# First routing in lots between attention tiles, and one expert's second products behind the last table product, in a fused attention and mixture kernel

## The chip, the cores and the metric

The kernel runs on one core of a Trainium2 chip. The core has a matrix engine (PE, with its weight loads as PEld), a vector engine (DVE), an activation engine (ACT), a general engine (POOL) and a queue engine (SP) that mostly starts transfers. The metric is the device time of one execution in microseconds (us), as the median of several runs.

## What is computed

The reference runs three stages in a row: an attention through 32 memory slots a head, a mixture of eight experts of which each token uses two, and a dense layer with a cosine gate.

```python
a = softmax(phi); k_m = a^T k; v_m = a^T v              # per batch and head, 32 slots
attn = softmax(q k_m^T / sqrt(64)); x = attn v_m        # 2304 tokens x 512
logits = x @ w_gate + log1p(exp(x @ w_noise)) * noise   # 2304 x 8
for e in range(8):                                      # the two best experts of each token
    h = np.maximum(x[mask] @ w1[e], 0.0)                # 512 -> 1024
    out[mask] += top2_w[mask, k, None] * (h @ w2[e])    # 1024 -> 512
h = out @ w_in; g = h * np.cos(h); return g @ w_out     # 512 -> 2048 -> 512
```

Every number is float32 outside. Inside, the expert and dense products are float16 in high and low parts, three products for one.

## The kernel before

The 2304 tokens are 18 tiles of 128. **The attention** makes the keys and values of four batches (k_gen) and then runs each tile through t_gen: scores sc on PE; maximum and difference (smx, sd) on DVE; exp on ACT; sum and reciprocal (ssm) on DVE, recorded as last["t7V"] for tile 7; the product d on POOL; two transposes pt on PE and their copy e2T on ACT; the products x on PE ("t7P"); the copy xs and the routing's logits on ACT ("t7A"); and a high and low half hl, which SP stores to xd. There is one x buffer, so x of a tile waits for the copy of the tile before. The values of the last batch go through the one PSUM bank "kt" as pk, pv and vn, and so do the sums of the first two weights.

**The routing** (route) runs twice, over the tokens of tiles 0 to 7 and of tiles 8 to 17. It is a chain on DVE with two short functions on ACT: two best experts, a rank product on PE (rank), and then tables: for each tile two one-hot matrices (ohp, oha) on DVE and two table products on PE (tab). From the table of the first run comes idxA, from both comes idxB. They drive the gathers of an expert's first part (two tiles of 128 tokens) and second part (three tiles): POOL gathers rows of xd into xg, SP transposes them into x. Then PE makes h (l1) and y (l2).

**Each weight** is loaded as float32 in two halves (raw), squared in four pieces on ACT (w_square, instructions junk), summed by PE (sum_up, sums) and turned into a scale on DVE (wnm, wnt, wsc). Then ACT writes four high parts (w_hi) and DVE four low parts (w_lo). Weights 0 and 1 are those of the first expert, w1 and w2.

**Order.** Every step is put on a line of times with at(t, ...), which gives it a priority; a scheduler then fixes the order on each engine. `gated(key)` forces an instruction behind a recorded one on the same engine, and `chain` keeps a kind of work in its order. So the first routing was one step at R0, put at the time of tile 13 with lots of 99; the pieces of both weights were gated behind tiles 7 to 17; and the y products of the first expert's first part were gated behind rank and the tables 2, 5 and 8:

```python
at(R0, advance, r0, 99)
at(tA + 0.01 + 0.001 * c, l2, 0, c, (("rank", "tab2"), ("tab5", "tab8"))[c], lead=LA)
```

In the profile most instructions that go through `chain` carry line 219, so one goes by their tiles.

## Time and profile before

| | us |
| --- | --- |
| median of 3 runs | 952.22 (951.37 to 953.31) |
| the profiled execution | 951.91 |
| its span, first to last instruction | 950.1 |
| PE busy in it | 894.6 |
| DVE, ACT, POOL busy | 583.9, 468.5, 213.1 |

The profile is one execution. Busy PE is not PE at its best: PEclk tells the share of the full clock that was granted in a stretch. Engines run side by side, and each takes its instructions in a fixed order, so an instruction can wait for something that it doesn't need because one ahead of it does. A row of a timeline has the start, the length, the engine, the line, the operation with the tiles written and read, the count, and in brackets the idle time before it and what ended that.

### The profile page before, as it was taken

What the parts mean: (1) busy time and instruction counts of PE and PEld (TensorE: products, weight loads), DVE (VectorE), ACT (ScalarE), POOL (GpSimd) and SP (SyncE); (2) the same over time, 40 slices, a digit from 0 to 9 for tenths busy, and PEclk for the clock granted to TensorE, in tenths of its full rate; (3) what the DMA queues carried; (4) which work ended last, traced back from release to release, by engine and by line L of the source; (5) the groups of instructions that cost most, each with busy time, mean ns of one, the idle gap of its engine ahead of it and who ended that gap; (6) DMA issues with size and microseconds to landing.
All of it is one profiled execution on the core that took longest, in us unless ns stands there. A gap on an engine that the chain in (4) does not pass through costs nothing. (4 is left out here: it accounts for less than half of the span.)

```text
span 950.1 us, 14147 instructions
## 1 busy us (share of the span) xinstructions
PE 894.6 (94%) x5368; PEld 521.2 (55%) x5368; DVE 583.9 (61%) x1266; ACT 468.5 (49%) x830; POOL 213.1 (22%) x234
## 2 busy tenths in 40 slices
PE   4996795999999999999998999989999999999997
PEld 3775463574746565564745555655444444444564
DVE  2568561385766567576763338887885774555564
ACT  3487523567666676667772324444433433332242
POOL 1353302201010201001000114443522432322222
PEclk8796597999999999999999999999999999999999
DMA  9972308858877879988753273231400320200010
GB/s 353 396 265 103 77 33 266 260 172 288 264 234 263 196 274 286 300 231 292 264 178 134 79 242 70 78 77 34 112 11 12 109 59 0 77 13 1 1 45 23
DMA packets 108246, 146.55 MB, mean 154 GB/s; under 512 B 65808, under 2 KB 66448, under 8 KB 106128
## 3 DMA queue, kind: packets, MB, share of 16 engines
q1 hardware_dynamic: 89536, 103.56, 35.1%
q0 software_dynamic: 6080, 19.93, 7.3%
q10 hardware_dynamic: 12560, 22.13, 6.6%
q8 instruction: 43, 0.70, 0.3%
q14 instruction: 27, 0.22, 0.1%
HBM read 95.26 MB, written 35.13 MB: 137 GB/s over the span
## 5 line engine op out<-in xcount | busy, mean ns | idle before, releaser
L219 PE MATMUL h<-x,w 128*128 128x384 f16 (+1 forms) x1536 | 216.0, 302 | 10.8 <-DMA x<-xg 10.6
L219 PE MATMUL y<-w,hT 128*128 128x512 f16 x960 | 212.7, 381 | 4.0 <-issue 4.0
L219 PE MATMUL g<-x2T,win 128*128 128x256 f16 (+1 forms) x1152 | 202.5, 326 | 5.3 <-DVE ty L1010 4.1
L219 PE MATMUL o<-wout,gT 128*128 128x512 f16 x864 | 202.0, 379 | 0.4 <-POOL gT L1012 0.2
L219 PEld LDWEIGHTS <-w 128*128 128x128 f16 x1536 | 151.9, 100 | 70.8 <-issue 13.9
L219 PEld LDWEIGHTS <-win 128*128 128x128 f16 x1152 | 112.6, 98 | 89.8 <-issue 7.6
L219 PEld LDWEIGHTS <-hT 128*128 128x128 f16 x960 | 94.3, 99 | 113.8 <-issue 6.6
L1012 POOL TENSOR_TENSOR gT<-ty,gT 128x256 f16<-128x256 f32 (+1 forms) x96 | 92.6, 965 | 252.9 <-ACT gT L1011 249.1
L1009 ACT ACTIVATE tt<-tt,hp 128x256 f32<-128x256 f32 (+1 forms) x96 | 58.9, 614 | 164.1 <-DVE tt L1008 150.1
L219 PEld LDWEIGHTS <-gT 128*128 128x128 f16 x864 | 84.2, 98 | 93.5 <-POOL gT L1012 2.2
L219 DVE SCALAR_TENSOR_TENSOR w<-raw,wsc,w 128x1024 f16<-128x1024 f32 x64 | 81.1, 1282 | 41.9 <-ACT w L219 38.3
L219 DVE SCALAR_TENSOR_TENSOR hT<-h,hT 128x384 f16<-128x384 f32 (+1 forms) x128 | 61.4, 487 | 66.6 <-ACT hT L219 66.0
L1006 DVE SCALAR_TENSOR_TENSOR ty<-g,wis,bct 128x256 f32<-128x256 f32 (+1 forms) x96 | 58.8, 612 | 65.7 <-PE g L219 65.7
L219 ACT ACTIVATE hT<-h 128x384 f16<-128x384 f32 (+1 forms) x128 | 55.4, 435 | 81.1 <-PE h L219 79.5
L1010 DVE SCALAR_TENSOR_TENSOR ty<-g,fac,tt 128x256 f32<-128x256 f32 (+1 forms) x96 | 59.1, 615 | 52.8 <-ACT tt L1009 52.1
L1011 ACT ACTIVATE gT<-ty 128x256 f16<-128x256 f32 (+1 forms) x96 | 50.2, 523 | 64.4 <-DVE ty L1010 64.3
L808 POOL DMA_INDIRECT xg<-xd,idxB x24 | 23.4, 974 | 219.9 <-DMA x<-xg 204.7
L219 ACT ACTIVATE w<-raw,wsc 128x1024 f16<-128x1024 f32 x64 | 71.6, 1140 | 2.2 <-ACT o L219 2.1
L1008 DVE SCALAR_TENSOR_TENSOR tt<-tt,ty 128x256 f32<-128x256 f32 (+1 forms) x96 | 68.9, 718 | 2.6
L219 ACT ACTIVATE junk<-raw 128x1024 bf16<-128x1024 f32 x64 | 67.5, 1054 | 3.9 <-ACT o L219 3.3
L219 ACT ACTIVATE o<-y,ysc 128x512 f32<-128x512 f32 x40 | 27.5, 686 | 75.9 <-PE y L219 64.8
L930 POOL DMA_INDIRECT y<-yd,sidx x36 | 36.1, 1003 | 91.4 <-DMA yd<-o 83.7
(234 smaller groups left out, 734.8 us busy)
## 6 DMA issues: line engine op xcount, KB each, us to landing
raw<-in_w SPq DMA_DIRECT2D x32, 1024.0 KB
yd<-o ACTq DMA_DIRECT2D x40, 256.0 KB
kvt<-in_kv SPq DMA_DIRECT2D x9, 1024.0 KB
cvt<-in_wi SPq DMA_DIRECT2D x8, 1024.0 KB
wst<-cvt SPq DMA_DIRECT2D x16, 512.0 KB
cvt<-in_wo SPq DMA_DIRECT2D x8, 1024.0 KB
yd<-zero ACTq DMA_DIRECT2D x13, 512.0 KB
xd<-hl SPq DMA_DIRECT2D x18, 256.0 KB
```

What stands on the lines that cost most here:

```text
L219: last[key] = fn(*a, **kw)
L808: G.indirect_dma_start(out=g, out_offset=None, in_=xd[0:NA * P] if part == 0 else xd, in_offset=bass.IndirectOffsetOnAxis(ap=idx[:, col:co ...
L930: G.indirect_dma_start(out=y, out_offset=None, in_=yd[0:rows], in_offset=bass.IndirectOffsetOnAxis(ap=sidx[:, t, k:k + 1], axis=0))
L1006: V.scalar_tensor_tensor(y, ph[:, :n], wis[:, 2 * E + c:2 * E + c + 1], bct[j], op0=OP.mult, op1=OP.mult)
L1008: V.scalar_tensor_tensor(t, t, MAGIC, y, op0=OP.subtract, op1=OP.subtract)
L1009: A.activation(t, t, AF.Sin, bias=hp, scale=-2.0 * math.pi)
L1010: V.scalar_tensor_tensor(y, ph[:, :n], fac[:, c:c + 1], t, op0=OP.mult, op1=OP.mult)
L1011: A.activation(g[:, 0, :n], y, AF.Copy)
L1012: G.tensor_tensor(g[:, 1, :n], y, g[:, 0, :n], op=OP.subtract)
```

## The change

The first routing is cut into lots (7, 7, 7 and the rest of its steps) at tiles 12 to 15, each lot gated behind that tile's reciprocal and behind the DVE half of the last batch's key copy. Of the first weight the squares go to tiles 7 to 10, the highs to 12 to 15, the lows behind the reciprocal of tile 17. Of the second weight the squares go behind the copies of tiles 16 and 17, the highs behind the Ln of the second routing and the lows behind idxB. The first expert's first y products go behind the last table product. The second half of the third weight's load is put behind the first gather.

```diff
@@ -436,7 +436,7 @@
             V.tensor_scalar(idxA, tb[:, :E * CA], float(TB), None, op0=OP.add)
             V.tensor_scalar(tabB, tb[:, E * CA:E * NST], float(TB), None, op0=OP.add)
         else:
-            V.tensor_tensor(idxB, tb[:, :nc_], tabB, op=OP.add)
+            last["idxB"] = V.tensor_tensor(idxB, tb[:, :nc_], tabB, op=OP.add)
         yield
         den = rg(g, "den", n)
         V.tensor_scalar(den, d, 1.0, eps, op0=OP.add, op1=OP.add)
@@ -596,7 +596,7 @@
         bk = bdk[b % 2]
         bdkt[b] = bk
         pv = pk[:, :2 * P].rearrange("p (c j m) -> p c j m", j=2, m=M)
-        V.tensor_copy(bk[0:64, :, 0:M], pv[0:64, :, 0, :])
+        last[f"bdk{b}V"] = V.tensor_copy(bk[0:64, :, 0:M], pv[0:64, :, 0, :])
         A.activation(bk[64:128, :, M:], pv[64:128, :, 1, :], AF.Copy)
         yield
         bv = ap.tile([P, 2, 272], F32, tag="bdv", name="bdv")
@@ -706,26 +706,32 @@
     k_start = (12.0, 23.0, 36.0, 46.0)
     k_steps = (-8.0, -4.0, 0.0, 4.0, 4.8, 5.4, 6.6, 7.2)
     e0_after = {
-        w_square: ("A", ((7, 7, 8, 8), (9, 9, 10, 11))),
-        w_hi: ("A", ((10, 11, 12, 12), (13, 14, 15, 16))),
-        w_lo: ("V", ((11, 12, 13, 13), (14, 15, 16, 17))),
+        (w_square, 0): ("t7A", "t8A", "t9A", "t10A"),
+        (w_hi, 0): ("t12A", "t13A", "t14A", "t15A"),
+        (w_lo, 0): ("t17V", "t17V", "t17V", "t17V"),
+        (w_square, 1): ("t16A", "t17A", "t17A", "t17A"),
+        (w_hi, 1): ("ln", "ln", "ln", "ln"),
+        (w_lo, 1): ("idxB", "idxB", "idxB", "idxB"),
     }
 
     def e0(fn, i, c):
 
-        k, after_t = e0_after[fn]
-        with gated(f"t{after_t[i][c]}{k}"):
+        with gated(e0_after[fn, i][c]):
             fn(i, c)
 
     def e0_scale(i):
-        with gated(f"t{(9, 12)[i]}P"):
+        with gated(("t11P", "t17P")[i]):
             sum_up(i, 4)
         norm_scale(i, 4)
 
-    def advance(gen, n):
-        for _ in range(n):
-            if next(gen, 1):
-                break
+    def advance(gen, n, *keys):
+
+        with ExitStack() as st:
+            for k in keys:
+                st.enter_context(gated(k))
+            for _ in range(n):
+                if next(gen, 1):
+                    break
 
     loads = [(load_phi, 0), (load_kv, 0, 2), (load_small,), (load_kv, 2, 4), (load_kv, 4, 6), (load_phi, 1),
              (load_q, 0, 4), (load_kv, 6, 10), (load_phi, 2), (load_q, 4, 8), (load_kv, 10, 14),
@@ -742,16 +748,20 @@
     for i in range(NT):
         stages(t_gen(i), [a_of(i) + x for x in t_steps])
     a_end = a_of(NT - 1) + 9.5
-    R0, R1, tA, LA = a_of(13), a_end - 0.5, a_end - 0.45, 60.0
+    R1, tA, LA = a_end - 0.5, a_end - 0.45, 60.0
     r0 = route(0)
-    at(R0, advance, r0, 99)
+    for t, n in ((12, 7), (13, 7), (14, 7), (15, 99)):
+        at(a_of(t) + 3.0, advance, r0, n, f"t{t}V", f"bdk{B - 1}V")
     whole(R1, route, 1)
-    for i in range(2):
-        for c in range(4):
-            at(a_of(e0_after[w_square][1][i][c]) + 8.5, e0, w_square, i, c)
-            at(a_of(e0_after[w_hi][1][i][c]) + 8.5, e0, w_hi, i, c)
-            at(a_of(e0_after[w_lo][1][i][c]) + 7.0, e0, w_lo, i, c)
-        at(a_of((9, 12)[i]) + 7.0, e0_scale, i)
+    for c in range(4):
+        at(a_of(7 + c) + 8.0, e0, w_square, 0, c)
+        at(a_of(12 + c) + 8.0, e0, w_hi, 0, c)
+        at(a_of(17) + 7.3 + 0.01 * c, e0, w_lo, 0, c)
+        at(a_of(17) + 8.0 + 0.01 * c, e0, w_square, 1, c)
+        at(tA + 0.0053 + 0.001 * c, e0, w_hi, 1, c)
+        at(tA + 0.0096 + 0.00001 * c, e0, w_lo, 1, c)
+    at(a_of(11) + 7.0, e0_scale, 0)
+    at(tA + 0.0047, e0_scale, 1)
 
 
     pools = {}
@@ -809,7 +819,7 @@
                                  in_offset=bass.IndirectOffsetOnAxis(ap=idx[:, col:col + 1], axis=0))
             if turn:
                 tr = SP.dma_start_transpose(out=xT[e, part][:, :, (c - c0) * P:(c - c0 + 1) * P], in_=g)
-        if (e, part) == (0, 1):
+        if e == 0:
             last["load"] = tr
 
     def turn_x(e, part, c):
@@ -1047,7 +1057,7 @@
         at(tA + 0.002 + 0.001 * f, l1, 0, 0, f, lead=LA)
         at(tA + 0.002 + 0.001 * f, l1_out, 0, 0, f, lead=LA)
     for c in range(CA):
-        at(tA + 0.01 + 0.001 * c, l2, 0, c, (("rank", "tab2"), ("tab5", "tab8"))[c], lead=LA)
+        at(tA + 0.01 + 0.001 * c, l2, 0, c, ((f"tab{NG - 1}",) * 2, ())[c], lead=LA)
         at(tA + 0.01 + 0.001 * c, l2_out, 0, c, lead=LA)
     ends, free = [], []
 
@@ -1174,7 +1184,7 @@
     put_weights(2 * E - 1, (x + 12.0, x + 15.0), x + 27.0, 0.0)
     for c in range(2 * NCH):
         put_chunk(c, X[1] + 2.0 + 18.5 * c)
-    put_weights(2, (tA - 12.0, tA - 0.01), X[0] + 1.0, 0.0)
+    put_weights(2, (tA - 12.0, tA + 0.0001), X[0] + 1.0, 0.0)
     put_weights(3, (X[0] + 4.0, X[0] + 8.0), X[0] + 17.0, X[1] + 1.5)
     for e in range(2, E):
         x = X[e - 1]
```

**Place 1, PE in the middle of the attention.** Before, from the sum of the first weight on: pk of the last batch, the rank products, x of tile 11 (x_1115) and the first half of tile 13's scores.

```order
L219 MATMUL sums_908<-wmx_109,ones32_111 128x5
L595 MATMUL pk_921<-ident_73,kd_902 128x128 x2
L390 LDWEIGHTS after_75
L390 MATMUL rank_1032<-m16_122,after_75 128x64
L391 LDWEIGHTS ones_77
L391 MATMUL rank_1032<-e32_83,ones_77 128x64
L392 LDWEIGHTS ones_77
L392 MATMUL rank_1032<-m16_122,ones_77 128x64
L681 MATMUL x_1115<-bdv_715,e2T_969 128x272 x2
L673 MATMUL pt_155<-ident_73,d_1109 128x128 x2
L610 MATMUL pv_941<-ident_73,vm_905 64x128 x2
L653 MATMUL sc_154<-bdk_141,qt_186 64x64 x4
```

Now, from x of tile 7 (x_795) to x of tile 9 (x_894):

```order
L681 MATMUL x_795<-bdv_440,e2T_763 128x272 x2
L673 MATMUL pt_155<-ident_73,d_789 128x128 x2
L595 MATMUL pk_911<-ident_73,kd_900 128x128 x2
L653 MATMUL sc_154<-bdk_139,qt_186 128x64 x4
L681 MATMUL x_865<-bdv_440,e2T_803 128x272 x2
L673 MATMUL pt_155<-ident_73,d_857 128x128 x2
L653 MATMUL sc_154<-bdk_139,qt_186 64x64 x4
L610 MATMUL pv_931<-ident_73,vm_903 64x128 x2
L653 MATMUL sc_154<-bdk_141,qt_186 64x64 x4
L653 MATMUL sc_154<-bdk_141,qt_186 128x64 x4
L681 MATMUL x_894<-bdv_715,e2T_873 128x272 x2
```

The last batch's pk and pv and the scores that need them moved from behind the weight's sum to between tiles 7 and 9.

**Place 2, DVE around idxA.** Before, with one-hot work, two low parts (w) and the tiles' smx, sd and ssm:

```order
L425 TENSOR_TENSOR oha<-acode,af_125 128x160
L431 TENSOR_SCALAR ohp<-iota_r,pf 128x128 x2
L219 SCALAR_TENSOR_TENSOR w<-raw,wsc,w 128x1024
L661 TENSOR_TENSOR sd_144<-sc,smx 128x8x32
L427 TENSOR_TENSOR oha<-oha,tokb 128x160
L431 TENSOR_SCALAR ohp<-iota_r,pf 128x128 x2
L658 TENSOR_REDUCE smx<-sc 128x8
L436 TENSOR_SCALAR idxA<-tab 128x16
L437 TENSOR_SCALAR tabB<-tab 128x24
L661 TENSOR_TENSOR sd_145<-sc,smx 128x8x32
L666 TENSOR_REDUCE ssm<-sd_144 128x8
L627 TENSOR_SCALAR sbt<-vn 128x1
```

Now, from the last but one pair of one-hot columns on; the reciprocal is that of tile 17:

```order
L431 TENSOR_SCALAR ohp<-iota_r,pf 128x128 x2
L667 RECIPROCAL ssm<-ssm 128x8
L219 SCALAR_TENSOR_TENSOR w<-raw,wsc,w 128x1024
L431 TENSOR_SCALAR ohp<-iota_r,pf 128x128 x2
L219 SCALAR_TENSOR_TENSOR w<-raw,wsc,w 128x1024
L427 TENSOR_TENSOR oha<-oha,tokb 128x160
L436 TENSOR_SCALAR idxA<-tab 128x16
L437 TENSOR_SCALAR tabB<-tab 128x24
L219 SCALAR_TENSOR_TENSOR w<-raw,wsc,w 128x1024 x2
```

All sums of the tiles moved ahead of idxA, and the four low parts stand together around it.

**Place 3, behind the attention.** ACT before, from the copy of tile 17:

```order
L685 ACTIVATE xs<-x,sT 128x512
L691 ACTIVATE rt<-x 128x32
L695 ACTIVATE hl<-xs 128x512
L352 ACTIVATE rt<-rt 128x80
L355 ACTIVATE rt<-rt 128x80
L219 ACTIVATE hT<-h 128x256 x5
```

ACT now, from the same copy; junk is a square of the second weight, w a high part of it:

```order
L685 ACTIVATE xs<-x,sT 128x512
L691 ACTIVATE rt<-x 128x32
L219 ACTIVATE junk,wmx<-raw 128x1024
L695 ACTIVATE hl<-xs 128x512
L352 ACTIVATE rt<-rt 128x80
L219 ACTIVATE junk,wmx<-raw 128x1024
L355 ACTIVATE rt<-rt 128x80
L219 ACTIVATE junk,wmx<-raw 128x1024
L219 ACTIVATE hT<-h 128x256 x4
L219 ACTIVATE w<-raw,wsc 128x1024
L385 ACTIVATE rt<-rt 128x10
L219 ACTIVATE hT<-h 128x256
```

Three squares stand ahead of the first hT now, and highs between the hT. On PE the last tables stood among the y products, ahead of the second part's h (x_1607 is its x):

```order
L219 LDWEIGHTS hT
L219 MATMUL y<-w,hT 128x512
L219 LDWEIGHTS hT
L219 MATMUL y<-w,hT 128x512
L432 LDWEIGHTS ohp
L432 MATMUL tab<-oha,ohp 128x24
L432 LDWEIGHTS ohp
L432 MATMUL tab<-oha,ohp 128x24
L219 LDWEIGHTS w
L219 MATMUL h<-x_1607,w 128x384
```

Now the tables come first:

```order
L432 LDWEIGHTS ohp
L432 MATMUL tab<-oha,ohp 128x24
L432 LDWEIGHTS ohp
L432 MATMUL tab<-oha,ohp 128x24
L219 LDWEIGHTS hT
L219 MATMUL y<-w,hT 128x512
L219 LDWEIGHTS hT
L219 MATMUL y<-w,hT 128x512
```

All 48 y products moved behind the last table product.

## Rows read from the trace of the kernel before

**Rows 1.** The profile's headline.

```profile
span 950.1 us, 14147 instructions
```

**Rows 2.** Timeline of PE, mid-attention: start, us, engine, line, operation, count [idle, releaser].

```profile
78.23 0.69 PE L595 MATMUL pk<-ident,kd 128*128 128x128 f32 x2 [1.73 <-DVE wnm L219]
...
84.74 1.18 PE L681 MATMUL x<-bdv,e2T 128*128 128x272 f32 x4 [0.80 <-ACT e2T L675]
...
89.58 1.73 PE L653 MATMUL sc<-bdk,qt 128*128 128x64 f32 x8 [2.61 <-DVE sd L661]
...
98.22 2.09 PE L681 MATMUL x<-bdv,e2T 128*64 128x272 f32 x8 [0.47 <-ACT e2T L675]
```

**Rows 3.** Timeline of PE, the attention's last tiles and the first expert product.

```profile
111.39 2.18 PE L681 MATMUL x<-bdv,e2T 128*128 128x272 f32 x4 [1.81 <-ACT e2T L675]
...
115.81 2.18 PE L681 MATMUL x<-bdv,e2T 128*128 128x272 f32 x4 [1.81 <-ACT e2T L675]
117.78 4.16 PE L219 MATMUL h<-x,w 128*128 128x256 f16 x24
```

**Rows 4.** Timeline of DVE while the first routing runs.

```profile
66.45 0.29 DVE L349 TENSOR_TENSOR rlgp<-rlgb 128x128 f32<-128x128 f32 x1 [0.90 <-ACT rlgb L691]
...
70.35 0.20 DVE L667 RECIPROCAL ssm<-ssm 128x8 f32<-128x8 f32 x1
...
72.72 1.08 DVE L362 TENSOR_TENSOR rl<-rl,rc 128x64 f32<-128x64 f32 x1
73.83 0.23 DVE L363 TENSOR_TENSOR rl<-rl,noise_sb 128x64 f32<-128x64 f32 x1
...
85.46 0.41 DVE L658 TENSOR_REDUCE smx<-sc 128x8 f32<-128x256 f32 x1
...
91.70 0.17 DVE L436 TENSOR_SCALAR idxA<-tab 128x16 int32<-128x16 f32 x1
```

**Rows 5.** Timeline of ACT: a square, a high part, and behind the last tile.

```profile
81.43 1.06 ACT L219 ACTIVATE junk<-raw 128x1024 bf16<-128x1024 f32 x1
...
114.33 1.15 ACT L219 ACTIVATE w<-raw,wsc 128x1024 f16<-128x1024 f32 x1
...
120.81 0.27 ACT L355 ACTIVATE rt<-rt 128x80 f32<-128x80 f32 x1 [1.01 <-DVE rt L354]
120.98 0.37 ACT L219 ACTIVATE hT<-h 128x256 f16<-128x256 f32 x1
```

**Rows 6.** Timeline of PE behind the attention.

```profile
128.68 0.30 PE L390 MATMUL rank<-m,after 128*128 128x80 f16 x1
...
139.89 2.75 PE L219 MATMUL y<-w,hT 128*128 128x512 f16 x12
142.48 0.20 PE L432 MATMUL tab<-oha,ohp 128*128 128x24 f16 x2
153.29 6.92 PE L219 MATMUL h<-x,w 128*128 128x384 f16 x27 [10.61 <-DMA x<-xg]
```

**Rows 7.** Timeline of DVE, the second routing's last two instructions.

```profile
137.62 0.20 DVE L427 TENSOR_TENSOR oha<-oha,tokb 128x48 f16<-128x48 f16 x1
142.72 0.18 DVE L439 TENSOR_TENSOR idxB<-tab,tabB 128x24 int32<-128x24 f32 x1 [4.90 <-PE tab L432]
```

**Rows 8.** Stretches: length, busy us (count) of PE PEld DVE ACT POOL, PEclk, DMA.

```profile
66.45:91.87 25.42, 16.04 (x99) 12.16 (x99) 22.10 (x78) 22.45 (x50) 9.52 (x12) 0.76 0.25 96
92.00:120.60 28.60, 21.89 (x76) 15.51 (x76) 16.07 (x36) 14.08 (x29) 11.99 (x12) 0.50 0.40 105
...
153.30:158.10 4.80, 4.80 (x16) 2.27 (x17) 0.25 (x1) 0.77 (x2) 1.30 (x2) 0.50 0.98 365
```

**Rows 9.** Timelines of POOL and DVE, later: gathers beside low parts.

```profile
175.52 0.94 POOL L808 DMA_INDIRECT xg<-xd,idxA  x1 [6.13 <-DMA x<-xg]
176.94 1.91 POOL L808 DMA_INDIRECT xg<-xd,idxA  x1 [0.47 <-issue]
...
173.16 4.87 DVE L219 SCALAR_TENSOR_TENSOR w<-raw,wsc,w 128x1024 f16<-128x1024 f32 x4 [0.48 <-ACT w L219]
```

## The prediction

> **What bounds the kernel now.** The profile's own time is 951.91 us, a span of 950.1 [rows 1] and 1.81 around it; the median of the runs is 952.22, 0.31 above. The sum is made against 951.91 and the 0.31 is added at the end. I read the timeline of PE first, since PE is busy for nearly the whole span, and look for where it stands still. There are two such places before 160 us. After them PE has work without a gap for hundreds of microseconds, so what is won before the product of the second token part starts (153.29, [rows 6]) should be kept to the end.
>
> The first place is the middle of the attention. The x products of tiles 12 and 13 start at 84.74 and 98.22 [rows 2], 13.48 apart. Later tiles start 4.42 apart (111.39, 115.81), with 1.81 idle before each, ended by ACT's e2T [rows 3]. The reason for the long one is in the other rows: the transpose pk of the last batch's keys stood until 78.23 and was released by DVE's wnm, the first instruction that reads the bank of the weight's sum. This wnm stands on DVE behind half of the first routing. Then sc stood for 2.61 until 89.58, released by DVE's sd [rows 2], which stands behind the table's one-hot work and a low part. DVE is busy 22.10 of the 25.42 from the routing's first instruction to idxA [rows 4, 8]: it runs the routing in one piece and the tiles wait behind it.
>
> The second place is behind the attention. idxB is ready at 142.72; DVE had finished its part at 137.82 and waited 4.90 for the last table product, which stood on PE behind y products [rows 6, 7]. Then PE has nothing for 10.61 until gather and transposes are done [rows 6], and the first 4.80 of the work after that run at PEclk 0.50, which is 1.2 GHz [rows 8].
>
> **Part one, the routing in lots.** Each lot waits for the sums of tile 12, 13, 14 or 15 on DVE. pk, pv and vn are moved on PE between tiles 8 and 11, ahead of the weight's sum, so the pk wait and the sc wait both lose their cause. What is late next is the tile's own chain: x, evacuation, a 1.15 or 1.06 weight instruction on ACT [rows 5], e2T, next x. That chain is the pitch of 4.42, measured with a high part in every tile and PE at 2.18 per x [rows 3]; now tiles 12 to 15 have a high part and tile 16 a square, about the same. I keep x of tile 12 at 84.74 and put five pitches behind it: x of tile 17 starts at 84.74 + 5 x 4.42 = 106.84 and ends at T = 109.0, where it was 117.99 (115.81 + 2.18). **Gain 9.0.**
>
> DVE must keep up with this. The routing now starts when tile 12's reciprocal is done, 70.55 instead of 66.45 [rows 4]. Of the 25.42 the 3.3 of idle go, and so do the instructions of tiles 11 and 12 that lay in it (about five of 0.41 and two of 0.20, 2.3). In come those of tiles 13 to 17, three of 0.41 and one of 0.20 each, 5 x 1.43 = 7.2, less three that were there already (1.2) [rows 4]: 25.42 - 3.3 - 2.3 + 6.0 = 25.8, and idxA would be ready at 96.4, against 91.70. The two low parts that stand ahead of idxA now are the two that stood there before. The last table products stand on PE ahead of x of tile 15, which by the pitch starts at 98.0, so DVE has 1.6 to lose in waits before the tiles feel it. The gather for the first expert's first part is then due, by the 10.57 from idxB to the product for three tiles [rows 6, 7] (there are two here), by 98.0 + 10.6 = 108.6, just below T. Ends: if the clock stays full, an x takes 1.18 (84.74, [rows 2]) and the pitch is 3.42, but idxA at 96.4 plus 10.6 holds the product to 107 or a little less for two tiles, a gain of 11 to 12. If the rank products, which now stand ahead of x of tile 12, or the lots come some 5 late, the gain is 4. I take 9.0, since PEclk was 0.50 from 92 to 120.6 [rows 8] with the same gaps per tile.
>
> Moved with it and costed at nothing: on POOL the two gathers of idxA now follow the last d and stand ahead of the hl of tiles 14 to 17; x evacuations wait for those buffers only three tiles later. On SP the second half of the third weight (its buffer is freed by the low parts of the first) stands behind the transposes, and the stores of tiles 15 to 17 behind it; only the gather of idxB needs these, more than 20 us after T. Without that cover each would add its own wait to the gather.
>
> **Part two, behind the attention,** counted from T. ACT gets three squares of the second weight ahead of the first hT, 3 x 1.06 = 3.2, of which 1.01 fills ACT's idle time there [rows 5]: the h banks are freed 2.2 later. Three high parts follow between the hT before the rank products: 1.15 + 0.37 = 1.52 a block, where PE's pitch was 1.35 (84 products or seven blocks from 117.78 to 128.68, the first two in 4.16, [rows 3, 6]): 0.5 more. So rank, which was at T + 10.7, comes at T + 13.4. From rank to idxB were 14.04; with no y product between the tables the 4.90 wait goes but for some 0.4 of table products: 9.5. idxB is ready at T + 22.9 (before T + 24.7).
>
> Now y follows the last table. Its second product needs the first low part, which DVE does right behind idxB: 0.18 and a quarter of 4.87 [rows 7, 9], T + 24.3. The following three lows take 1.22 each against 1.4 for the products that use one. The y products are 4 x 2.75 = 11.0 [rows 6] at full clock. Between the last h block and this place PE has only the tables for nearly 8 us, so I take it that the clock has fallen and the first 4.8 run at half, which costs 2.4 [rows 8]. y ends at T + 24.3 + 11.0 + 2.4 = T + 37.7. The gather is ready at T + 22.9 + 10.6 = T + 33.5 and lies under it. The next product starts at T + 37.7 where it started at T + 35.3 (153.29 - 117.99): **2.4 lost.** But PE comes to it from 13 us of y, warm, so the 4.80 at half clock [rows 8] are not paid there: **2.4 won back.** Part two comes out at nothing; its ends are 5 lost (y at half clock to its end, or lows that lag) and 4 won (clock never falls).
>
> What hides the gather is y, with 4.2 to spare. In a later stage two gathers were issued beside four low parts: the first took 0.94, the second 1.91 [rows 9]; so 1 to 3 of the spare is used. The Trainium skill (SBUF — State Buffer, section "SBUF: two separate sides") says that DVE and GpSimd take a shared port pair as an exclusive lock for a whole instruction, and that a DMA issued from GpSimd cannot have its descriptors written while DVE holds it. The 1.91 agrees in direction, while the 0.94 beside the same low parts does not. By that rule all three gathers could wait for all four lows, 4.9 later, 0.7 beyond the end of y, and the time would be 943.9.
>
> **Sum:** 951.91 - 9.0 + 2.4 - 2.4 = 942.9, with the 0.31 **943** to the median.
>
> **The rivals.** (a) The clock stays full through the tiles. For it: PE now does pk, sc and vn of the last batch and the sums between tiles 8 and 12, where it stood. Against it: 1.81 idle in each pitch. Then part one gives 11 to 12 and part two 2.4, about 938.
> (b) The lots hold the tiles. A one-lot routing blocked sd once; four lots in DVE's queue can block it four times, and a 128x64 instruction took 1.08 where its neighbour took 0.23 [rows 4]. POOL now has d and hl of five more tiles beside the lots; at 0.85 a hit, five or six hits make x of tile 15 wait 3 to 5. The Trainium skill's lock rule (same page and section) works in this direction too. Gain 4 to 5, about 948.
> (c) Slower: the weight work that lay under the attention's tiles lies open behind them. Three squares, four highs and four lows are 3.2 + 4.6 + 4.9 = 12.7; less the 1.0 of idle and the 4.5 of freed table wait this is 7.2 added if h, tables and y do not cover the highs and lows. It decides from the point where part one brings less than 7.2; with 3 from part one the time is 956.
> (d) The change doesn't reach its aim: the rank products ahead of x of tile 12 wait for DVE as long as pk and sc did, and the 13.48 only move to another tile. Then parts one and two are near nothing, 951 to 953.
>
> **How the numbers follow.** 0.2% of 952 is 1.9 us, about what can be told from no change. The forecast (939.5 to 947) has 0.60, (a) 0.15, (b) 0.14, (d) 0.06, (c) 0.05. Faster is the forecast with (a) and (b), 0.89; same is (d), 0.06; slower is (c), 0.05. The range from 935 to 950 takes in the ends of both parts and most of (a) and (b), and leaves out (c), (d) and a little of the others, under 0.2.
>
> **What would show it.** In the changed profile: no wait of pk on wnm and of sc on sd; x of tiles 12 and 13 within 6 us; idxA at 95 to 99, after x of tile 14; x of tile 17 ending at 106 to 112; rank 12 to 15 behind that; no wait of idxB above 1 us; no wait of the second part's h on a DMA, and PEclk 1.00 when it starts, near 146.7. It is wrong if x of tile 15 waits for tables, if ACT's highs hold the h banks for long, or if y is late at half clock and the gain of part one is given back there.

## The result

The changed kernel takes 940.84 us in the median of four runs (937.86 to 943.83), the kernel before 951.8 beside it (949.94 to 953.31). The ratio is 0.9886, with a 95% interval of 0.9849 to 0.9923: 11.0 us or 1.1% faster. Forecast were 943 in a range of 935 to 950. Single runs of one kernel lie up to 7.6 us apart here, so medians and intervals are compared below, and where a profile is read, distances within it.

The profiled run of the changed kernel is the slowest of its four (943.83); its headline answers to [rows 1].

```profile
span 942.0 us, 14143 instructions
```

The timeline of PE, mid-attention to the last tile, answers to [rows 2, 3]. The columns are start, duration, engine, line, operation, names, tile, count, and the idle time before it with what ended it.

```profile
66.16 1.14 PE L681 MATMUL x<-bdv,e2T 128*128 128x272 f32 x4
67.35 0.38 PE L595 MATMUL pk<-ident,kd 128*128 128x128 f32 x2
...
73.71 1.10 PE L653 MATMUL sc<-bdk,qt 128*128 128x64 f32 x8 [1.28 <-DVE sd L661]
...
82.46 0.28 PE L219 MATMUL sums<-wmx,ones 128*128 128x5 f32 x2
...
85.58 2.11 PE L681 MATMUL x<-bdv,e2T 128*128 128x272 f32 x4
...
90.24 2.09 PE L681 MATMUL x<-bdv,e2T 128*64 128x272 f32 x8 [2.11 <-ACT e2T L675]
...
99.19 0.29 PE L432 MATMUL tab<-oha,ohp 128*128 128x40 f16 x4 [2.00 <-DVE oha L427]
99.32 2.16 PE L681 MATMUL x<-bdv,e2T 128*128 128x272 f32 x4
...
108.13 2.18 PE L681 MATMUL x<-bdv,e2T 128*128 128x272 f32 x4 [1.81 <-ACT e2T L675]
```

The x products of tiles 12 and 13 (85.58, 90.24) are 4.66 apart instead of 13.48. pk (67.35) stands right behind tile 7 and waits for nothing; the sum, which stood ahead of it, follows at 82.46. x of tile 17 ends at 110.31, where it ended at 117.99.

Two more rows of the kernel before, from its timeline of PE: x of tile 7, and the second part's product with its first 72 products in one row.

```profile
64.47 1.14 PE L681 MATMUL x<-bdv,e2T 128*128 128x272 f32 x4
...
153.29 14.23 PE L219 MATMUL h<-x,w 128*128 128x384 f16 x72 [10.61 <-DMA x<-xg]
```

The timeline of PE behind the attention, answering to [rows 6]:

```profile
110.10 3.38 PE L219 MATMUL h<-x,w 128*128 128x256 f16 x24
116.14 1.47 PE L219 MATMUL h<-x,w 128*128 128x256 f16 x12 [2.66 <-DVE hT L219]
...
122.83 0.30 PE L390 MATMUL rank<-m,after 128*128 128x80 f16 x1
...
127.48 0.51 PE L432 MATMUL tab<-oha,ohp 128*128 128x24 f16 x6 [2.86 <-DVE oha L427]
...
132.66 8.05 PE L219 MATMUL y<-w,hT 128*128 128x512 f16 x23 [1.06 <-DVE w L219]
141.49 5.34 PE L219 MATMUL y<-w,hT 128*128 128x512 f16 x24 [0.78 <-ACT o L219]
146.67 11.86 PE L219 MATMUL h<-x,w 128*128 128x384 f16 x72
```

The second part's product starts at 146.67 without a wait, where it started at 153.29 after 10.61 of idle. The wait of 10.61 is gone, but three smaller ones have come: on hT, on the tables, on the first low part. Of the first 24 y products the last 23 stand here, and they run slow: 8.05, against 5.34 for the next 24.

The timeline of DVE of the changed kernel, answering to [rows 4, 7], and behind it that of ACT, answering to [rows 5]:

```profile
99.52 0.17 DVE L436 TENSOR_SCALAR idxA<-tab 128x16 int32<-128x16 f32 x1 [0.38 <-PE tab L432]
...
131.21 0.18 DVE L439 TENSOR_TENSOR idxB<-tab,tabB 128x24 int32<-128x24 f32 x1 [0.29 <-PE tab L432]
```

```profile
114.23 1.04 ACT L219 ACTIVATE junk<-raw 128x1024 bf16<-128x1024 f32 x1
115.27 0.64 ACT L219 ACTIVATE hT<-h 128x256 f16<-128x256 f32 x2
```

idxB waits 0.29 instead of 4.90. On ACT the squares of the second weight (the "junk" rows, the last of which stands here) are ahead of hT at 115.27, which PE waits for.

The stretches (length, busy us and count of PE, PEld, DVE, ACT, POOL, then the granted clock, the DMA share and GB/s), answering to [rows 8]:

```profile
92.00:110.00 18.00, 11.71 (x42) 7.66 (x41) 10.97 (x18) 10.41 (x21) 10.61 (x8) 0.50 0.41 109
...
147.00:152.00 5.00, 5.00 (x32) 3.03 (x31) 1.12 (x2) 3.31 (x6) 0.00 (x0) 1.00 1.04 399
```

The tiles still run at the 1.2 GHz level. The second part's product now starts at the 2.4 GHz level: its first 72 products take 11.86. In the kernel before the same 72 took 14.23, so 2.37 are won there.

Up to that product the changed kernel is 153.29 - 146.67 = 6.62 ahead, with the 2.37 it is 8.99. At the end of the two profiles 8.1 of this are left (spans of 950.1 and 942.0). In this run the x product of tile 7 already stood 1.69 later (66.16 against 64.47), in a stretch the change hardly touches; other profiles below have it anywhere from 63.4 to 66.4.

### The profile page after: what moved, and what is told of

The parts are those of the page before. It is cut to its first block, busy times and chain, and to the rows that moved or that the text cites. A ratio compares the mean times of both kernels' runs of the same rounds, so it can differ in the third digit from the quotient of the medians.

```text
span 942.0 us, 14143 instructions
## 1 busy us (share of the span) xinstructions
PE 889.7 (94%) x5368; PEld 515.1 (55%) x5368; DVE 584.2 (62%) x1266; ACT 468.1 (50%) x830; POOL 216.4 (23%) x234
## 5 line engine op out<-in xcount | busy, mean ns | idle before, releaser
L219 PE MATMUL y<-w,hT 128*128 128x512 f16 x960 | 215.8, 385 | 5.4 <-issue 3.6
L219 PE MATMUL h<-x,w 128*128 128x384 f16 (+1 forms) x1536 | 213.0, 300 | 2.7 <-DVE hT L219 2.7
L219 DVE SCALAR_TENSOR_TENSOR hT<-h,hT 128x384 f16<-128x384 f32 (+1 forms) x128 | 61.4, 486 | 65.3 <-ACT hT L219 63.4
## 6 DMA issues: line engine op xcount, KB each, us to landing
raw<-in_w SPq DMA_DIRECT2D x32, 1024.0 KB, 11.5
```

Source lines behind the costliest of these rows:

```text
L219: last[key] = fn(*a, **kw)
```

## The experiments

Two distances in each profile carry the reading: A, from the start of x of tile 7 to the end of x of tile 17, and B, from there to the start of the second part's h product.

| kernel | A | B | median us | ratio to before, 95% interval |
|---|---|---|---|---|
| before | 53.52 | 35.30 (then 2.37 cold) | 951.8 | |
| changed | 44.15 | 36.36 | 940.84 | 0.9886 [0.9849, 0.9923] |
| e1 one piece | 43.40 | 35.42 | 939.60 | 0.9875 [0.9857, 0.9892] |
| e2 lots only | 53.73 | 41.36 (then cold) | 957.39 | 1.0059 [1.0044, 1.0075] |
| e3 gate of y only | 52.58 | 31.88 | 945.77 | 0.9937 [0.9923, 0.9952] |
| e12 sum's place only | 49.88 | 35.04 (then 1.74 cold) | 949.67 | 0.9987 [0.9973, 1.0000] |
| e14 sum's place and gate | 52.11 | 33.08 | 946.08 | 0.9941 [0.9923, 0.9959] |
| e16 split and gate | 47.47 | 34.96 | 944.64 | 0.9930 [0.9912, 0.9949] |
| e11 one piece, lows earlier | 43.37 | 35.11 | 939.16 | 0.9862 [0.9836, 0.9888] |
| e5 squares behind Ln | 43.51 | 37.54 | 941.85 | 0.9907 [0.9884, 0.9930] |
| e9 and the sum behind rank | 44.29 | 33.05 | 936.85 | 0.9872 [0.9841, 0.9903] |
| e4 filled tables | 44.95 | 33.42 | 937.43 | 0.9868 [0.9841, 0.9896] |
| e6 filled attention | 48.27 | 35.62 | 944.82 | 0.9930 [0.9910, 0.9951] |
| e10 combined | 43.41 | 33.96 | 937.86 | 0.9857 [0.9838, 0.9876] |

"Cold" is what 72 products of the second part take above 11.86; for e2 no row shows them alone.

A is not the same each time, even where nothing in the attention differs. The kernel before and e3 have the same instructions in the same order on PE, ACT, DVE and POOL up to the last x, and so have e12 and e14, and the changed kernel, e4, e5 and e9. Their A is 53.52 and 52.58, 49.88 and 52.11, and 43.51 to 44.95. So a difference of about 2 in A between two profiles shows nothing by itself. The profiled run of e12, 946.84, is also 2.8 below that kernel's median.

### Do the lots clear the tiles?

The change taken back for the lots alone:

```diff
-    for t, n in ((12, 7), (13, 7), (14, 7), (15, 99)):
-        at(a_of(t) + 3.0, advance, r0, n, f"t{t}V", f"bdk{B - 1}V")
+    at(a_of(13), advance, r0, 99)
```

> The changed kernel with the first routing issued in one piece again (no waits of lots on the sums of tiles 12 to 15); the moved weight pieces and the gate of y stay. The lots theory (the routing in lots ends the gap between the x products of tiles 12 and 13): the gap is back at 12 to 13.5, x of tile 12 to the end of x of tile 17 is about 33 (24.7 in the changed kernel), time 949 to 951. The weight theory (the gap goes because pk, pv and vn now stand on PE ahead of the weight's sum and the low parts are gone from between the tiles): tiles 12 and 13 within 6, x of tile 12 to the end of tile 17 24 to 26, pk without a wait on wnm, time 939 to 943. If each takes away one of the two waits (pk on wnm, sc on sd), the gap is 7 to 9 and the time 944 to 947.

The timeline of PE with the routing in one piece:

```profile
83.21 1.18 PE L681 MATMUL x<-bdv,e2T 128*128 128x272 f32 x4
...
86.63 2.09 PE L681 MATMUL x<-bdv,e2T 128*64 128x272 f32 x8 [2.01 <-ACT e2T L675]
```

Tiles 12 and 13 are 3.42 apart, and the time is 939.6, at the level of the changed kernel. The lots theory falls: once the rest of the change is there, the routing may be issued in one piece, and A is no longer (43.40 against 44.15).

The other way round, the kernel before with the lots and the load order that goes with them:

```diff
...
-    at(R0, advance, r0, 99)
+    for t, n in ((12, 7), (13, 7), (14, 7), (15, 99)):
+        at(a_of(t) + 3.0, advance, r0, n, f"t{t}V", f"bdk{B - 1}V")
...
-        if (e, part) == (0, 1):
+        if e == 0:
...
-    put_weights(2, (tA - 12.0, tA - 0.01), X[0] + 1.0, 0.0)
+    put_weights(2, (tA - 12.0, tA + 0.0001), X[0] + 1.0, 0.0)
```

> The kernel before with the routing in lots alone; the weights' pieces and the gates of y as before. The lots theory: tiles 12 and 13 within 6, the end of x of tile 17 about 9 earlier, time 942 to 945. The weight theory: the low parts and the sum still stand between the tiles, so the table products come after x of tile 16 or 17 and idxA after 105 (91.70 before, 99.52 in the changed kernel); what the tiles win, the first expert's product then loses waiting for the gather, which takes 10.6 behind idxA: time 949 to 956.

The timelines of this kernel, first DVE with the routing's first instruction and idxA, then PE with x of tiles 16 and 17 and the first expert's product:

```profile
79.25 0.27 DVE L349 TENSOR_TENSOR rlgp<-rlgb 128x128 f32<-128x128 f32 x1
...
117.67 0.17 DVE L436 TENSOR_SCALAR idxA<-tab 128x16 int32<-128x16 f32 x1 [0.66 <-PE tab L432]
```

```profile
107.70 2.18 PE L681 MATMUL x<-bdv,e2T 128*128 128x272 f32 x4 [2.02 <-ACT e2T L675]
...
117.97 2.18 PE L681 MATMUL x<-bdv,e2T 128*128 128x272 f32 x4 [0.34 <-ACT e2T L675]
126.50 5.81 PE L219 MATMUL h<-x,w 128*128 128x256 f16 x36 [6.36 <-DMA x<-xg]
```

It is 0.6% slower than the kernel before. The lots wait for the copy of pk, and pk still stands behind the sum: the routing starts at 79.25 (66.45 in [rows 4]), idxA is ready at 117.67 (91.70), and the first expert's product waits 6.36 for the gather. The tiles themselves don't gain either (A is 53.73): tiles 12 and 13 are closer, 9.91 apart (85.29 and 95.20), but the gap has moved, and tile 17 stands 10.27 behind tile 16. Its reciprocal comes on DVE at 114.94, behind the last lot's one-hots.

### What does clear them?

The change moves two other things among the tiles: the place of the first weight's sum, and the second weight's pieces, which go behind the attention (the split). e3 has neither, e14 the first, e16 the second, e1 both; all four have y behind the last table and the routing in one piece. e1 differs from the other three in one thing more: the first weight's squares, high and low parts are at later tiles, the high parts one to a tile.

The gate of y alone:

```diff
-        at(tA + 0.01 + 0.001 * c, l2, 0, c, (("rank", "tab2"), ("tab5", "tab8"))[c], lead=LA)
+        at(tA + 0.01 + 0.001 * c, l2, 0, c, ((f"tab{NG - 1}",) * 2, ())[c], lead=LA)
```

> The kernel before with one edit: y of the first part behind the last table product instead of between the tables. By the terms of the prediction: the 4.90 wait of idxB goes but for 0.4, gather B is ready 4.5 earlier, y (11.0 at full clock, 13.4 with a cold start) hides it, the second part's product starts 1.6 to 4 earlier and warm (2.4): 946 to 949 for a kernel of 952. Rival (the wait only changes place: y now ends as late as the gather did): 951 to 953. If it gives 3 to 6, then the second weight's pieces behind the attention cost about as much in the changed kernel, where part two came out at nothing.

PE of this kernel, the second part's start:

```profile
148.00 11.86 PE L219 MATMUL h<-x,w 128*128 128x384 f16 x72
```

B falls from 35.30 to 31.88, and the 2.37 of the cold start go: 3.42 + 2.37 = 5.8, and the median falls by 5.9, to just below the 946 to 949 that were expected. One line brings about half of what the whole change brings.

The place of the sum alone, on the kernel before:

```diff
-        w_hi: ("A", ((10, 11, 12, 12), (13, 14, 15, 16))),
-        w_lo: ("V", ((11, 12, 13, 13), (14, 15, 16, 17))),
+        w_hi: ("A", ((11, 11, 12, 12), (13, 14, 15, 16))),
+        w_lo: ("V", ((12, 12, 13, 13), (14, 15, 16, 17))),
...
-        with gated(f"t{(9, 12)[i]}P"):
+        with gated(f"t{(11, 12)[i]}P"):
...
-        at(a_of((9, 12)[i]) + 7.0, e0_scale, i)
+        at(a_of((11, 12)[i]) + 7.0, e0_scale, i)
```

> The kernel before with PE's product for the first weight's sum behind x of tile 11 instead of tile 9, and, because they need it, the first high part and the first low part behind tiles 11 and 12 instead of 10 and 11. Routing in one piece, the second weight under the attention, y between the tables as before. Theory (the 13.48 between x of tiles 12 and 13 came from that sum standing ahead of pk, pv and vn): tiles 12 and 13 within 6, x of tile 7 to the end of x of tile 17 44 to 47 (53.5 before, 43.4 to 44.2 with the moved weights); part two as before, 35.3 behind that end: 943 to 946. Rival (the low parts and the second weight's pieces between the tiles hold the tables and sd all the same): 948 to 952.

> That place of the sum together with the gate of y (5.9 lower than the kernel before when alone), and nothing else of the change: routing in one piece, the second weight under the attention. Theory (the two add up, and lots and split are not needed for them): the part of the run before this one and 5.9 more, 937 to 940, as low as the changed kernel or lower. If the second weight's pieces under the attention cost 2 to 4 of pitch, 941 to 944, and the split behind the attention is then what the changed kernel wins by.

Both theories that promised a full gain miss. The timelines of e12 ahead of x of tile 13, of PE, ACT and DVE in this order (the first of two low parts stands; the last row is where the second weight's scale begins):

```profile
84.07 2.18 PE L681 MATMUL x<-bdv,e2T 128*128 128x272 f32 x4 [0.52 <-ACT e2T L675]
...
93.03 0.70 PE L432 MATMUL tab<-oha,ohp 128*128 128x40 f16 x4 [2.04 <-DVE ohp L431]
93.67 2.09 PE L681 MATMUL x<-bdv,e2T 128*64 128x272 f32 x8
```

```profile
83.96 2.19 ACT L219 ACTIVATE w<-raw,wsc 128x1024 f16<-128x1024 f32 x2
...
88.25 2.18 ACT L219 ACTIVATE w<-raw,wsc 128x1024 f16<-128x1024 f32 x2
90.33 0.37 ACT L675 ACTIVATE e2T<-pt 128x256 f32<-128x256 f32 x1
```

```profile
89.13 1.27 DVE L219 SCALAR_TENSOR_TENSOR w<-raw,wsc,w 128x1024 f16<-128x1024 f32 x1
...
93.94 0.15 DVE L219 TENSOR_REDUCE wnm<-sums 128x1 f32<-128x5 f32 x1
```

pk waits no longer (it runs at 64.74), but tiles 12 and 13 are still 9.60 apart. ACT has four high parts between two e2T, so e2T of tile 13 comes at 90.33; DVE has two low parts of 1.27 between the one-hots, so the table products ahead of x of tile 13 come at 93.03. All six are parts of the first weight: the edit puts them behind tiles 11 and 12, and the second weight has no scale before its wnm at 93.94. Of the second weight only one square (1.04 at 86.05 on ACT) stands here. The rows of e1 to compare with these are the only high part ahead of e2T of tile 13 on ACT, and the first low part on DVE:

```profile
85.16 1.15 ACT L219 ACTIVATE w<-raw,wsc 128x1024 f16<-128x1024 f32 x1
```

```profile
92.98 1.23 DVE L219 SCALAR_TENSOR_TENSOR w<-raw,wsc,w 128x1024 f16<-128x1024 f32 x1
```

This e2T comes at 86.20, and the first low part only when x of tile 14 (91.59) has started. So once pk is free, tile 13 waits for the first weight's own pieces. With the gate, e14 gives no more than the gate alone gave (946.08 against 945.77); its A is 2.2 longer than that of e12 with the same order of instructions.

The split without the sum's place, on e1:

```diff
-        (w_square, 0): ("t7A", "t8A", "t9A", "t10A"),
-        (w_hi, 0): ("t12A", "t13A", "t14A", "t15A"),
-        (w_lo, 0): ("t17V", "t17V", "t17V", "t17V"),
+        (w_square, 0): ("t7A", "t7A", "t8A", "t8A"),
+        (w_hi, 0): ("t10A", "t11A", "t12A", "t12A"),
+        (w_lo, 0): ("t11V", "t12V", "t13V", "t13V"),
...
-        with gated(("t11P", "t17P")[i]):
+        with gated(("t9P", "t17P")[i]):
...
```

> The one-piece kernel with the first weight's pieces and sum where the kernel before has them (sum behind x of tile 9, ahead of pk; squares behind tiles 7 and 8, highs behind 10 to 12, lows behind 11 to 13); only the second weight's pieces lie behind the attention, and y behind the last table. With the runs so far it fills a table of two by two, all with that gate of y: neither move 945.8, the sum's place alone 946.1, both 939.6, and here the split alone. Theory A (the split alone clears the tiles, the sum's place is worth nothing): x of tile 7 to the end of tile 17 43 to 45, time 938 to 941. Theory B (each wait hides the other, so only both together bring it): pk waits on wnm behind the routing as before, x of tile 7 to the end of tile 17 50 to 53, time 946 to 950, since part two still pays for the split. Between: 942 to 945.

The timeline of PE of this kernel, pk and x of tiles 12 and 13:

```profile
78.68 0.69 PE L595 MATMUL pk<-ident,kd 128*128 128x128 f32 x2 [1.73 <-DVE wnm L219]
...
83.77 1.18 PE L681 MATMUL x<-bdv,e2T 128*128 128x272 f32 x4 [0.43 <-ACT e2T L675]
...
94.22 2.09 PE L681 MATMUL x<-bdv,e2T 128*64 128x272 f32 x8 [0.47 <-ACT e2T L675]
```

pk waits for wnm at 78.68 as in [rows 2], and tiles 12 and 13 are 10.45 apart. The time, 944.64, lies between the two theories. So in A, against e3's 52.58: the sum's place takes 0.5 off (e14; 3.6 in e12 against the kernel before, so its size is not settled), the split 5.1, and e1 with both 9.2. In the medians: 945.77 with neither, 946.08, 944.64, and 939.60 in e1. The split alone brings only 1.1 there, since it pays 3.1 in B (34.96 against 31.88), and the sum's place nothing that can be told. Together, in e1, they bring 6.2: behind the first wait stands another, and what one move frees, the next wait holds.

One piece of that is left unparted: e1 has the first weight's pieces later too, and by the rows of e12 it is these that hold tile 13 once pk is free. So the 6.2 belong to the sum's place, the split and the later pieces of the first weight together. For the low parts there is a run, on e1:

```diff
-        (w_lo, 0): ("t17V", "t17V", "t17V", "t17V"),
+        (w_lo, 0): ("t13V", "t14V", "t15V", "t16V"),
...
-        at(a_of(17) + 7.3 + 0.01 * c, e0, w_lo, 0, c)
+        at(a_of(13 + c) + 7.3, e0, w_lo, 0, c)
```

> The one-piece kernel with the low parts of the first weight back between the tiles (behind the sums of tiles 13 to 16 instead of 17). It parts the two moves of the first weight: the sum behind pk, pv and vn, and the low parts. If the sum's place is all: the x products of tiles 12 and 13 stay within 6, idxA comes 1 to 3 later, time 939 to 941. If the low parts matter too: x of tile 13 or 15 waits for the tables behind them, idxA 4 to 6 later, the first expert's product waits on the gather for 1 to 4, time 941 to 945.

A is 43.37, the median 939.16: no difference. Only the first low part moved far, though (to 88.38, from 92.98 in e1); two stand ahead of idxA in both. What the high parts of the first weight cost by themselves, and so how the gain of e1 over e14 divides between the two weights, stays open.

### What does the split cost behind the attention?

With both weights under the attention B is 31.88 (e3) or 33.08 (e14), with the split from 34.96 (e16) to 36.36 (changed). The difference is 1.9 to 4.5. The waits named above show where it lies; three runs take them one by one. First the squares:

```diff
-        (w_square, 1): ("t16A", "t17A", "t17A", "t17A"),
+        (w_square, 1): ("t16A", "ln", "ln", "ln"),
...
-        at(a_of(17) + 8.0 + 0.01 * c, e0, w_square, 1, c)
+        at(tA + 0.004 + 0.0001 * c if c else a_of(17) + 8.0, e0, w_square, 1, c)
```

> The changed kernel with three squares of the second weight behind the second routing's Ln on ACT instead of ahead of it and of the first hT. Theory (the squares hold both hT, for which PE waited 2.66, and exp and Ln, for which DVE's routing waited 1.1): the wait of h on hT falls under 0.8, rank stands 11 to 12 behind the end of x of tile 17 (12.52 in the changed kernel), idxB 19 to 20 behind (20.9), time 1 to 2 lower, 939 to 940. Rival (the high parts come as much later and hold the h banks or the low parts, so that y's second product waits longer than 1.06): within 0.5 of the changed kernel, or up to 1 slower.

The timeline of PE behind the attention, with the squares moved:

```profile
110.72 1.47 PE L219 MATMUL h<-x,w 128*128 128x256 f16 x12 [0.37 <-DVE hT L219]
116.06 0.59 PE L219 MATMUL sums<-wmx,ones 128*128 128x5 f32 x2 [3.87 <-ACT junk L219]
```

The wait on hT falls from 2.66 to 0.37, as expected, and PE then stands 3.87 at the product of the second weight's sum, which needs the last square. Rank comes 14.32 behind the end of tile 17 instead of 12.52, and the time is 941.85, no lower than that of the changed kernel. The rival had named the high parts; it was PE's own queue. So the same kernel with the sum behind rank:

```diff
-        with gated(("t11P", "t17P")[i]):
+        with gated(("t11P", "rank")[i]):
```

> The kernel with the second weight's squares behind Ln (run before this one), and with PE's product for that weight's sum behind the second routing's rank products. In that run the wait on hT fell from 2.66 to 0.37, but PE then stood 3.87 at the product of the sum, which waited for the last square. Theory (the squares cost time only through what is queued behind them on ACT and PE): without that wait rank stands 10.5 to 11.5 behind the end of x of tile 17, idxB 18.5 to 19.5 behind (19.1 where the whole second weight lay under the attention), time 2 to 3 lower than that run and 1 to 2 lower than the changed kernel: 938 to 940. Rival (the high parts, now later, hold hT and the h banks, or the low parts): 941 to 943.

The same stretch of PE with the sum behind rank:

```profile
117.27 0.30 PE L390 MATMUL rank<-m,after 128*128 128x80 f16 x1 [4.60 <-DVE m L382]
...
129.71 5.12 PE L219 MATMUL y<-w,hT 128*128 128x512 f16 x23 [1.86 <-DVE w L219]
...
140.79 11.86 PE L219 MATMUL h<-x,w 128*128 128x384 f16 x72
```

B is 33.05, and the median 936.85, 4 under the changed kernel and 5 under e5. Rank stands 9.53 behind tile 17 (expected 10.5 to 11.5), though it waits 4.60 for DVE's routing; h products that are left over fill the time between the tables, and y starts warm: 5.12 for the same 23 products. What stays is the wait of 1.86 for the first low part.

Then the clock alone, with products that keep PE busy:

```diff
...
+    at(tA + 0.0098, fill, "P", 10, lead=LA)
+    at(tA + 0.0099, fill, "tab5", 5, lead=LA)
```

> The changed kernel with 15 products added whose result nothing reads (128x512 fp16: ten behind the first expert's last h product, five behind the second table group), so that PE does not stand before y. It measures the cold start of y. Theory (y's first half runs cold because PE had only tables before it): these 23 products, 8.05 in the changed kernel, fall to 5.2 to 6, y ends 2 to 3 earlier behind the end of x of tile 17 (36.5), the second part's product still waits for no DMA, time 938 to 939. Rival (the added products hold the tables, so idxB comes later by about what y wins): the same as the changed kernel. Third: gather B is then ready behind the end of y, and the product waits on a DMA for up to 2: within 1 of the changed kernel.

PE with the added products (L1066) ahead of the tables:

```profile
122.51 2.32 PE L1066 MATMUL dm<-ones 128*128 128x512 f16 x10
...
130.71 5.12 PE L219 MATMUL y<-w,hT 128*128 128x512 f16 x23 [1.27 <-DVE w L219]
...
141.78 11.86 PE L219 MATMUL h<-x,w 128*128 128x384 f16 x72
```

The 23 products take 5.12 instead of 8.05: the cold start of y is 2.9 in this pair of profiles. Without added products the same 23 took 7.10 in e1 and 6.80 in e11, so it is 1.7 to 2.9. B falls by 2.94 and the median by 3.4. The gather is not late: idxB was ready at 129.25, the product starts 12.53 later and waits for no DMA.

The filled attention was meant to hold the clock through the tiles:

```diff
+        if 9 <= t <= 16:
+            dm = trp("dm")
+            for _ in range(6):
+                T.matmul(dm.rearrange("p (a b) -> p a b", b=P), lhsT=ones,
+                         rhs=ones[:, None, :].to_broadcast([P, 4, P]), start=True, stop=True)
```

> The changed kernel with six products added behind x of each of the tiles 9 to 16 (128x512 fp16, into a bank that nothing reads), so that PE stands less between the tiles. It tests the prediction's rival of a full clock. Theory (the pitch of 4.42 contains x at half clock; at full clock it is 3.42): the stretch from tile 13 on runs at a granted clock near 1.00, x of tile 12 to the end of tile 17 falls from 24.7 to 20 to 22, but idxA then stands nearer to that end and the first expert's product waits on the gather, so that 1 to 3 of it stay, time 938 to 940. Rival (the added products stand in PE's queue ahead of the table products and of x, the clock does not rise for good): 941 to 945.

Stretches of this kernel, in the columns of the stretches above:

```profile
66.00:88.00 22.00, 21.62 (x151) 15.12 (x149) 14.92 (x51) 14.37 (x39) 8.86 (x11) 1.00 0.23 89
...
94.00:114.00 20.00, 14.49 (x50) 9.44 (x50) 10.71 (x26) 11.12 (x23) 10.26 (x8) 0.50 0.53 140
```

It failed for the question asked. All added products were issued ahead of x of tile 12; up to 88 PE was busy for 21.62 of 22.00 at the 2.4 GHz level, and from 94 on, without them, the tiles ran at the 1.2 GHz level again. What the added products cost (A is 4.1 longer) was for nothing. What the tiles would take at full clock to their end is open; one step of it stands in e1, where x of tile 12 took 1.18 and tile 13 followed after 3.42.

Last, e1, e5 and e9 in one kernel:

> A version from the runs: the changed kernel with the routing in one piece, three squares of the second weight behind Ln, and PE's product for its sum behind the rank products. The kernel with the last two was 936.85 and the one-piece kernel 1.2 under the changed one. If both add up: 935 to 936.5. If the routing's pieces don't matter: 936.5 to 938.

937.86, in five runs from 937.15 to 938.99. The two gains don't add up, and one piece or lots makes no difference here either. e4, e9 and e10 have medians 3 to 4 below the changed kernel, but their intervals overlap with its wide one (0.9849 to 0.9923), and e4 and e9 each had runs above 943; the shorter B in all three profiles is the firmer sign.

## Why the prediction was right, point by point

**The sum.** 942.9 was expected for the profiled run, which took 943.83; 943 for the median, which is 940.84. Up to the second part's product, part one gave 9.37 for 9.0 and part two 1.31 for nothing, and the later start took 1.69 back; 0.9 more went behind that product. So the sum came out near, but part one in part for a wrong reason, and that is luck.

**Part one, 9.0.** A fell by 9.37 (53.52 to 44.15). T, the end of x of tile 17, is 110.31 and not 109.0, since tile 7 stood 1.69 later in this run; from x of tile 12 to T it is 24.73, where 24.28 were put down. idxA, expected at 96.4 to 98, came at 99.52, or 97.83 without that shift. The pitch of 4.42 from one x to the next holds in the last tiles. x of tile 15 did wait for tables (2.00 at 99.19), which the prediction had named as a sign of failure; it cost 0.3, as it starts 4.74 behind tile 14.

**What was wrong in it** is the step "Part one, the routing in lots", as far as it credits the lots. It lists two lost waits, pk on wnm and sc on sd, and says that the lots and pk's place ahead of the sum end them. e1 shows that the lots bring nothing, and e2 that alone they cost 5.7. The step also let the moved weight pieces pass with "about the same" for the tiles: it counted one high part in each tile after the change, not the pairs of high parts and the low parts between the one-hots that go away. With e1, the runs e12, e14 and e16 show that the gain comes from the sum's place and the moved pieces of the weights, and that together they bring more than apart (9.2 of A against 0.5 and 5.1); which of the pieces bring how much stays open. The step's number came out because the new pitch was read from tiles that had already been free of all of this.

**Part two, nothing.** B rose by 1.06 (35.30 to 36.36) where 2.4 were expected, and the warm start gave 2.37 where 2.4 were expected. Its terms: rank T + 12.52 (expected 13.4; the high parts cost the h blocks nothing, 48 products in 5.40), idxB T + 20.9 (22.9: from rank to idxB 8.38 instead of 9.5), y's second product T + 22.35 (24.3), its cold start 1.7 to 2.9 (2.4), and its end T + 36.5 (37.7). The wait on hT (2.66) and y's wait for a low part (1.06) were in the sum, as 2.2 and as the quarter of the lows. e3 and e9 show what the prediction could not part: the gate by itself gives 5.8, and the split takes 1.9 to 4.5 of it back.

**The cover.** The gather lies under y. In e4 12.53 from idxB to the product were enough; in the changed kernel it was 146.67 - 131.21 = 15.46, so at least 2.9 were spare (4.2 less 1 to 3 were expected). The case of 943.9, in which all three gathers wait for all four low parts, did not come: the first took 1.80, the others 0.94 and 0.95.

**The rivals.** (a) did not come: the clock was 0.50 from 92 to 110. (b) did not: sc waited for sd 1.28 at 73.71 and 0.74 at 83.76, and no more behind that, and the tables' wait cost 0.3 and not 3 to 5. (c) has its mechanism and not its size: the split lies open with 1.9 to 4.5, not 7.2, and part one pays for it. (d) did not: rank stands directly ahead of x of tile 12 and holds it for nothing. In e2, with the lots alone, the gap does move to another tile, but to tile 17 and behind one-hots.

## What to carry to other kernels

Where several instructions stand behind one wait, take away one cause and look at what is queued next before you credit it: here two moves brought nothing and 1.1 us alone, and 6.2 together in a kernel that also moved what stood behind them. Undo each part of a change by itself; the part that the change was named for brought nothing, and alone it made the kernel slower. A product that only feeds a later step (a weight's sum here) should not stand in TensorE's queue ahead of work that is ready, and work kept for the time between small products spares the next stage a cold start.

## What the runs showed of the hardware

A low part on DVE takes 1.27 in most places. Beside two hl of POOL it took 3.22 in the changed kernel; the timeline of POOL stands first, that of DVE second:

```profile
103.27 2.28 POOL L696 TENSOR_TENSOR hl<-xs,hl 128x512 f16<-128x512 f32 x2
```

```profile
103.42 3.22 DVE L219 SCALAR_TENSOR_TENSOR w<-raw,wsc,w 128x1024 f16<-128x1024 f32 x1 [2.44 <-ACT w L219]
```

The low part ends with the second hl and a low part's length more: 103.27 + 2.28 + 1.27 is 106.82, and it ended at 106.64. The Trainium skill (SBUF — State Buffer, section "SBUF: two separate sides") says that the two engines share a port pair and that an instruction takes it as an exclusive lock, on DVE one with two inputs in SBUF, as here, against one of POOL that reads SBUF. This pair of rows agrees with it. That gathers wait for low parts, as the prediction took it, is seen only in part, in the timeline of POOL of the changed kernel:

```profile
131.66 1.80 POOL L818 DMA_INDIRECT xg<-xd,idxB  x1 [5.49 <-DVE idxB L439]
133.77 0.94 POOL L818 DMA_INDIRECT xg<-xd,idxB  x1 [0.30 <-issue]
```

Here the four low parts ran on DVE from 131.33 to 136.28. The gather that started behind the first of them took 1.80, the next two, under the same low parts, 0.94 and 0.95; the first took 1.80 in e1, e4 and e5 too. In e9, where the first gather started 0.25 ahead of the low parts, the three took 0.98, 1.07 and 0.95. Why only the first is delayed was not tried.
